# The first batch's keys and scores in another order, by key blocks, in a fused attention and adapter kernel

## The chip, the cores and the metric

The kernel runs on one core of a Trainium2 chip, as one program. The metric is the device time of one execution in microseconds (us). Engines named below: TensorE (PE in the profile, PEld for its weight loads), VectorE (DVE), ScalarE (ACT), GpSimd (POOL) and SyncE (SP), which only issues transfers. Each engine works through its own queue of instructions; semaphores order them against each other.

## The reference

Four images of 384 x 32 pixels with 128 channels are average-pooled by 4 x 4 patches and projected, which gives 768 keys that are also the values. 12,288 queries for each image attend to them. The result goes through a mixture of eight rank-16 adapters, of which each row uses its two best.

```python
def _attn_ref(q, kv, w_sr):
    kv_pool = kv.reshape(B, H // r, r, W // r, r, C).mean(axis=(2, 4))
    kv_flat = kv_pool.reshape(B, -1, C) @ w_sr
    k = v = kv_flat
    s = scale * (q @ k.transpose(0, 2, 1))
    s = s - s.max(-1, keepdims=True)
    a = np.exp(s)
    a /= a.sum(-1, keepdims=True) + 1e-09
    return (a @ v).astype(np.float32)

def _moe_ref(x, w_gate, A, B):
    logits = x @ w_gate
    topk = np.argpartition(-logits, K, axis=1)[:, :K]      # K = 2
    w = softmax of the two selected logits
    delta[row] += w[row, k] * ((x[row] @ A[e]) @ B[e])     # for the two experts e
    return x + delta
```

B = 4, C = 128, r = 4, q is 4 x 12,288 x 128, kv is 4 x 384 x 32 x 128, all fp32; the output is 49,152 x 128 fp32.

## The kernel before

**Chunks and slots.** The 49,152 queries are cut into 96 chunks of 512 (24 for each image, which the code calls a batch). The main loop (line 417) has a slot for each chunk k from 4 to 95. In slot k the scores of chunk k are computed in three pairs of key blocks, `scores(k, 0)` to `scores(k, 2)` (line 238): two bf16 matmuls of 128 x 512 into one of two PSUM buffers (`sg`), then ScalarE's exponential into `em[k]`. `attend(k, s)` (line 248) multiplies `em[k]` with the values `vx`, six matmuls of 137 columns for each of four row groups, into `acc`, of which there is one buffer (`ps_a`, line 62). `normalize` (line 256) reads `acc` on VectorE, a reciprocal and a multiply into `xn`. `top` and `route` (lines 276, 285) find the two best experts and their weights, with a tanh on ScalarE. Then a chunk enters the adapter stage: `transposes` of `xn`, `down`, `gate` on VectorE, transposes of `hg` one slot later, `up` and `finish` (the store, issued by SP) one slot after that. The dictionary `att` (line 400) says which chunks attend in which slot; from chunk 8 on chunk k attends in slot k + 1, and before that chunk 0 has slot 4, chunk 1 slot 5, and slots 6, 7 and 8 have two each. `enter` follows from it.

**The start.** Chunks 0 to 3 have their scores computed ahead of the loop (lines 369 to 386), between the steps that make the first batch's keys. The first batch's pixels come in thirds h = 0, 1, 2 of two key blocks each. A third is loaded by eight transfers of 256 KB on SP's queue, `load_kv(0, h, r, x)` (line 89), r the row inside a patch and x which of the two key blocks; before, the order is r outer, x inner. `pair_step` (line 173) adds two rows on VectorE (512 columns); `keys` (line 187) sums the rest of a patch by 16 accumulating fp32 transposes on TensorE and scales it out of PSUM by VectorE into `kpT`; `keys2` (line 203) projects with `w_sr` and VectorE casts the result to `kfT`; `values` (line 209) makes `vx`, with the eight gate logits as extra columns. In the loop of line 372 the four adds of a third come together, then its 16 transposes, and between them the scores of the third before and its values.

**Queries.** The queries of chunks 0 to 7 are loaded as fp32 and turned on TensorE by `turn_q(g, m, engine)` (line 107): four transposes and one cast of 512 columns out of PSUM by the engine named. Chunks 0 to 3 (g = 0) are cast by ScalarE, and so are chunks 4 to 7 (g = 1, lines 397 and 454). From chunk 8 on queries come by a casting transfer on POOL's queue (`cast_q`) and a transposing one on SP's (`load_qT`).

**Order.** Every instruction is marked with `keep`, so that it stays in program order on its engine. Small PSUM tiles (`mtile`, line 70) share two buffers, in turn. `part` (line 517) is an attention over some of the key blocks only; before, only the tail uses it.

Of the kernel before, what the change touches and what calls it, by code (L numbers as in the profile page):

```python
# [10 lines left out]
FP32 = mybir.dt.float32  # L11
BF16 = mybir.dt.bfloat16
U16 = mybir.dt.uint16
FP16 = mybir.dt.float16
AF = mybir.ActivationFunctionType
ALU = mybir.AluOpType
# [4 lines left out]
def kernel(  # L21
# [10 lines left out]
    nc = tc.nc  # L32
    P = 128
    B, N, C = q.tensor.shape
# [3 lines left out]
    J = NKV // P  # L38
    T = 512
    S = T // P  # L40
    GC = 4
    GT = GC * T
    VC = C + E
    VE = VC + 1
    NB = N // T
# [21 lines left out]
    def mm(*a, **k):  # L67
        return keep(nc.tensor.matmul(*a, **k))  # L68

    def mtile(shape, dtype=FP32, name="mb"):  # L70
        return ps_m.tile(shape, dtype, tag="mb", name=name)
# [52 lines left out]
    keep(nc.scalar.dma_start(w_gate_sb, moe_w_gate))  # L124
    load_q(0, 0, GC * S)
    for h in range(3):
        for r in range(4):
            for x in range(2):
                load_kv(0, h, r, x)
    for m in range(GC):  # L130
        load_q(1, m * S, m * S + S)
    b_f = const.tile([P, C], FP32)
# [22 lines left out]

    kfT, vx = {}, {}

    def prepare(b, adder):

        sums, rest = [], []  # L160

        def pool_step(h, step, lo, hi):
            t = kvr[b, h]
            if step < 3:
                u, v = t[:, 0].rearrange("p g c -> p (g c)"), t[:, step + 1].rearrange("p g c -> p (g c)")
            else:
                w = 2 * C if step == 3 else C
                u, v = t[:, 0, :, 0:w], t[:, 0, :, w:2 * w]
                keep(adder.tensor_tensor(u, u, v, op=ALU.add))  # L169
                return  # L170
            keep(adder.tensor_tensor(u[:, lo:hi], u[:, lo:hi], v[:, lo:hi], op=ALU.add))  # L171

        def pair_step(h, r, x):
            u, v = (kvr[b, h][:, r + i, x] for i in range(2))
            keep(adder.tensor_tensor(u, u, v, op=ALU.add))

        for h in range(3):
            if adder is nc.vector:
                sums.append([lambda h=h, r=r, x=x: pair_step(h, r, x)
                             for r in (0, 2) for x in range(2)])  # L180
                continue
            sums.append([lambda h=h, step=step, lo=lo: pool_step(h, step, lo, lo + 512)
                         for step in range(5) for lo in range(0, 1024 if step < 3 else 512, 512)])

        st = {}

        def keys(h):
            if h == 0:
                st["kpT"] = prep.tile([P, J, P], FP32, tag="kpT", name="kpT")
                kfT[b] = per_b.tile([P, J, P], BF16, tag="kfT", name="kfT")  # L190
            kpT = st["kpT"]
            ps = mtile([P, 2, P], name="kpT_ps")
            if adder is nc.vector:
                parts = [(r, i, c) for r in (0, 2) for i in range(2) for c in range(4)]
            else:
                parts = [(0, i, 0) for i in range(2)]
            for n, (r, i, c) in enumerate(parts):
                mm(ps[:, i], kvr[b, h][:, r, i, c * C:(c + 1) * C], id_f, is_transpose=True,
                   start=(n == 0), stop=(n == len(parts) - 1))
            keep(nc.vector.tensor_scalar(kpT[:, 2 * h:2 * h + 2], ps, 1.0 / 16.0, None,  # L200
                                         op0=ALU.mult))

        def keys2(h):
            kpT = st["kpT"]
            ps = mtile([P, 2, P], name="kfT_ps")
            mm(ps, w_sr_sb, kpT[:, 2 * h:2 * h + 2], start=True, stop=True)
            keep(nc.vector.tensor_copy(kfT[b][:, 2 * h:2 * h + 2], ps))

        def values(h):
            if h == 0:  # L210
                vx[b] = per_b.tile([P, J, VE], FP16, tag="vx", name="vx")
                keep(nc.vector.memset(vx[b][:, :, VC:VE], 1.0))
            ps = mtile([P, 2, VC], name="v_ps")
            for i in range(2):
                mm(ps[:, i], st["kpT"][:, 2 * h + i], wext, start=(i == 0), stop=(i == 1))
            keep(nc.vector.tensor_copy(vx[b][:, 2 * h:2 * h + 2, 0:VC], ps))
            if adder is not nc.vector:
                st["vb", h] = prep.tile([P, 2, C], BF16, tag="vb", name="vb")
                keep(nc.vector.tensor_copy(st["vb", h], ps[:, :, 0:C]))

        def turn(h):
            ps = mtile([P, 2, P], BF16, name="kfT_ps")
            for i in range(2):
                mm(ps[:, i], st["vb", h][:, i], id_bf, is_transpose=True,
                   start=(i == 0), stop=(i == 1))
            keep(nc.vector.tensor_copy(kfT[b][:, 2 * h:2 * h + 2], ps))

        for h in range(3):
            for f in (keys, keys2, values) if adder is nc.vector else (keys, values, turn):
                rest.append(lambda h=h, f=f: f(h))  # L230
        return sums, rest

# [133 lines left out]

    LA = 4

    for m in range(GC):
        turn_q(0, m, nc.scalar)  # L370
    sums, rest = prepare(0, nc.vector)
    for h in range(3):
        for item in sums[h]:
            item()
        rest[3 * h]()
        if h > 0:
            scores(2, h - 1)
        rest[3 * h + 1]()
        if h > 0:
            scores(3, h - 1)  # L380
            rest[3 * h - 1]()
        scores(0, h)
        scores(1, h)
    rest[8]()
    scores(2, 2)
    scores(3, 2)
    rest = []

    late = const.tile([P, 1], FP32)
    keep(nc.gpsimd.tensor_copy(late, q_f[1][:, GC * S - 1, 0:1]))  # L390
# [3 lines left out]
    keep(nc.vector.tensor_scalar(a_bf, a_f, 0.5, None, op0=ALU.mult))  # L394
    b_bf = const.tile([P, C], BF16)
    keep(nc.vector.tensor_copy(b_bf, b_f))
    turn_q(1, 0, nc.scalar)


    att = {LA: [0], LA + 1: [1], LA + 2: [2, 3], LA + 3: [4, 5], LA + 4: [6, 7]}  # L400
    for k in range(8, NCHUNK):
        att[k + 1] = [k]
    normed = {}
    for t, ks in att.items():
# [12 lines left out]
    for k in range(LA, NCHUNK):  # L417
        b, i = divmod(k, NB)
        ka = att.get(k, [])
        kx = enter.get(k, [])  # L420
        if k % GC == 0:
            g = k // GC
            if 2 <= g + 1 < B * NG:
                load_qT(g + 1)
            if 4 <= g + 2 < B * NG and g + 2 not in q_bf:
                cast_q(g + 2)
        if b + 1 < B:
            if i == 4:
                sums, rest = prepare(b + 1, nc.gpsimd)
            if 4 <= i < 16:  # L430
                h, j = divmod(i - 4, 4)
                load_kv(b + 1, h, j, None)

        def after_norm(kn):
            top(kn)
            if kn == first[kn] + size[kn] - 1:
                route(first[kn])

        kn = [n for n in att.get(k - 1, []) if normed[n] == k]
        if k == LA:  # L440
            for s in range(S):
                attend(0, s)
            ka = []
        scores(k, 0)
        while later:
            later.pop(0)()
        for n in kn:
            normalize(n)
        pairs = [(kx[j] if j < len(kx) else None, kh[j] if j < len(kh) else None)
                 for j in range(max(len(kx), len(kh)))]  # L450
        for x_, h_ in pairs[:1]:
            transposes(x_, h_)
        if k + 1 in range(GC + 1, 2 * GC):
            turn_q(1, (k + 1) % GC, nc.scalar)
        scores(k, 1)
        for u_ in ku:
            up(u_)
            finish(u_)
        for a_ in ka[:-1]:
            for s in range(S):  # L460
                attend(a_, s)
            normalize(a_)
            after_norm(a_)
        if ka and len(ka) == 1:
            attend(ka[0], 0)
        for n in kn:
            after_norm(n)
        scores(k, 2)
        for x_ in kx[:1]:
            down(x_)  # L470
            gate(x_)
        if rest and i in (14, 15, 16, 18, 19, 20, 21, 22, 23):
            rest.pop(0)()
        for a_ in ka[-1:]:
            for s in range(1 if len(ka) == 1 else 0, S):
                attend(a_, s)
        for x_, h_ in pairs[1:]:
            transposes(x_, h_)
        for x_ in kx[1:]:
            down(x_)  # L480
            gate(x_)
        ku = kh
        kh = kx
        if b + 1 < B and 10 <= i < 21:
            h, j = divmod(i - 10, 4)
            for _ in range((4, 3, 1, 0)[j]):
                sums[h].pop(0)()
# [24 lines left out]
    def fetch(which, k):  # L512
        sb = run.tile([P, S, P], BF16, tag="tt1", name="tt1")
        keep(nc.scalar.copy(sb, which[k]))
        which[k] = sb

    def part(k, o, js):
        for s in range(S):
            for j in js:
                mm(o[:, s, 0:VE], em[k][:, j, s * P:(s + 1) * P], vx[k // NB][:, j],  # L520
                   start=(j == 0 and s % 2 == 0), stop=(j == J - 1 and s % 2 == 1))

    def wide(o):
        return o.rearrange("p a b -> p (a b)")[:, 0:T].rearrange("p (s c) -> p s c", s=S)
# [147 lines left out]
```

## Time and profile before

| | us |
|---|---|
| three runs | 408.81, 409.08, 409.26; median 409.08 |
| the profiled run | 409.56, its span 407.6 |
| TensorE matmul busy | 379.6 (93%) |
| TensorE weight loads busy | 306.9 (75%) |
| VectorE busy | 324.5 (80%) |
| ScalarE busy | 293.1 (72%) |
| GpSimd busy | 170.7 (42%) |

The span is the time from the first to the last instruction of one profiled execution. Busy times overlap between engines. A line of a timeline gives the start, the time to the end of the last of the merged instructions, the engine, the line of the kernel (L68 is the helper behind every matmul), the operation, the tiles out<-in, the shapes, how many, and in brackets the time the engine stood idle before and what ended it. The granted clock of TensorE has a mean of 0.991 over the run.

### The profile page before, as it was taken

The page shows a single profiled execution, that of the slowest core. Times are in us where ns is not written, and L with a number is a line of the kernel's source. Part 1 is how long each engine was busy: PE and PEld are TensorE (multiplying, and loading weights), DVE is VectorE, ACT ScalarE, POOL GpSimd, SP SyncE. Part 2 cuts the span into 40 slices and gives each one's busy share as a digit, 9 for nine tenths or more (in the row PEclk, how much of TensorE's full clock was granted, in tenths as well). Part 3 has the DMA queues.
Part 4 walks back from the last instruction along what each step waited for, and adds up shares of the span by engine and source line. Part 5 has one row for each costly group of instructions (what it writes and reads, how often), then busy time and mean ns, then how long its engine had stood idle before and what let it go on. Part 6 is the DMA issues. An engine that isn't in the chain of part 4 may idle for free.

```text
span 407.6 us, 11369 instructions
## 1 busy us (share of the span) xinstructions
PE 379.6 (93%) x4514; PEld 306.9 (75%) x4589; DVE 324.5 (80%) x948; ACT 293.1 (72%) x346; POOL 170.7 (42%) x289
## 2 busy tenths in 40 slices
PE   3798899999999999999999999999999999898992
PEld 2556778788888788888888788878888878677781
DVE  2553678888888888989888888988988888887873
ACT  2389468767678777867778877876777877665772
POOL 0010128888512319879411319879311322123342
PEclk9999999999999999999999999999999999999996
DMA  8998568984855999994855979996756548252213
GB/s 297 366 265 245 137 156 214 285 210 124 182 130 105 307 172 336 295 219 138 168 130 117 363 103 344 287 225 145 156 131 149 138 130 156 79 138 97 79 53 132
DMA packets 71319, 76.45 MB, mean 188 GB/s; under 512 B 49921, under 2 KB 50433, under 8 KB 70785
## 3 DMA queue, kind: packets, MB, share of 16 engines
q1 hardware_dynamic: 70128, 63.98, 53.8%
q0 software_dynamic: 704, 11.54, 16.7%
q8 instruction: 36, 0.59, 0.6%
q10 hardware_dynamic: 432, 0.20, 0.2%
q14 instruction: 19, 0.15, 0.1%
HBM read 50.53 MB, written 36.70 MB: 214 GB/s over the span
## 4 chain that ended last, share of the span: by engine, by line
PE 82%; DVE 7%; ACT 3%; DMA 3%; issue 2%; SPq 1%; POOL 1%; ACTq 0%; DVEq 0%; POOLq 0%
PE acc L68 34%; PE sg L68 23%; PE tt_ps L68 10%; PE h_ps L68 6%; PE d_ps L68 5%; ACT em L246 2%; DVE rinv L258 1%; DVE xn L263 1%; DMA kvr<-in_kv_dram 1%; SPq L98 1%; DMA w_sr_sb<-in_w_sr_dram 1%; PE kpT_ps L68 1%; DVE tts L333 1%; PE v_ps L68 1%; DVE hg L347 1%
## 5 line engine op out<-in xcount | busy, mean ns | idle before, releaser
L246 ACT ACTIVATE em<-sg 128x1024 f16<-128x1024 f32 x288 | 279.1, 1023 | 92.1 <-PE sg L68 59.5
L68 PE MATMUL acc<-vx,em 128*128 128x137 f16 x2280 | 171.7, 224 | 1.7 <-DVE xn L263 1.6
L68 PE MATMUL sg<-qT,kfT 128*128 128x512 bf16 x501 | 154.7, 378 | 2.7 <-ACT em L246 2.2
L68 PEld LDWEIGHTS <-em 128*128 128x128 f16 x2304 | 149.6, 98 | 4.0 <-DVE xn L263 2.2
L68 PEld LDWEIGHTS <-tts 128*128 128x128 bf16 x740 | 56.4, 98 | 45.8 <-DVE tts L333 2.1
L293 POOL TENSOR_TENSOR over<-xn,srt 128x128 f32<-128x128 f32 (+2 forms) x62 | 21.4, 365 | 157.0 <-DVE srt L281 157.0
L347 DVE TENSOR_TENSOR hg<-h_ps,gw 128x512 bf16<-128x512 f32 x93 | 64.2, 691 | 13.2 <-POOL gw L315 7.6
L263 DVE TENSOR_TENSOR xn<-acc,rinv 128x544 f32<-128x544 f32 x95 | 68.8, 725 | 3.3
L333 DVE COPY tts<-tt_ps 128x1024 bf16<-128x1024 bf16 (+1 forms) x96 | 64.4, 671 | 3.6 <-PE tt_ps L68 3.6
L171 POOL TENSOR_TENSOR kvr<-kvr 128x512 f32<-128x512 f32 x54 | 66.7, 1271 | 0.0
L360 DVE TENSOR_TENSOR osb<-d_ps,xn 128x512 f32<-128x512 f32 x91 | 62.6, 691 | 0.5 <-PE d_ps L68 0.5
L68 PEld LDWEIGHTS <-kfT 128*128 128x128 bf16 x576 | 45.9, 97 | 6.0 <-issue 3.7
L68 PEld LDWEIGHTS <-xn 128*128 128x128 bf16 x384 | 29.4, 98 | 22.0 <-ACT xn L585 0.5
L258 DVE RECIPROCAL rinv<-acc 128x4 f32<-128x4 f32 x95 | 17.3, 182 | 32.5 <-PE acc L68 31.4
L68 PE MATMUL h_ps<-a_bf,tts 128*128 128x128 bf16 x372 | 36.0, 219 | 2.8 <-DVE tts L333 1.6
L68 PE MATMUL tt_ps<-id_bf,xn 128*128 128x128 bf16 x372 | 35.9, 219 | 1.5
L68 PE MATMUL d_ps<-b_bf,tts 128*128 128x128 bf16 x364 | 35.2, 219 | 2.3 <-DVE tts L333 1.3
L68 PE MATMUL tt_ps<-id_bf,hg 128*128 128x128 bf16 x368 | 35.6, 219 | 0.3 <-DVE hg L347 0.3
L281 DVE MAX8 srt<-xn 128x8 f32<-128x8 f32 x380 | 34.3, 153 | 0.2
L314 POOL TENSOR_TENSOR gw<-th,over 128x128 f32<-128x128 f32 (+2 forms) x31 | 12.0, 389 | 39.2 <-ACT th L312 39.1
L68 PEld LDWEIGHTS <-hg 128*128 128x128 bf16 x384 | 25.5, 98 | 2.5 <-issue 1.1
L169 POOL TENSOR_TENSOR kvr<-kvr 128x512 f32<-128x512 f32 (+1 forms) x18 | 18.1, 1006 | 0.9
(77 smaller groups left out, 174.8 us busy)
## 6 DMA issues: line engine op xcount, KB each, us to landing
out_dram<-osb SPq DMA_DIRECT2D x95, 256.0 KB, 3.3
kvr<-in_kv_dram SPq DMA_DIRECT2D x36, 512.0 KB, 6.3
qbf<-in_q_dram POOLq DMA_DIRECT2D x22, 512.0 KB, 6.1
kvr<-in_kv_dram SPq DMA_DIRECT2D x24, 256.0 KB, 5.4
qf<-in_q_dram SPq DMA_DIRECT2D x1, 1024.0 KB, 5.1
qf<-in_q_dram SPq DMA_DIRECT2D x4, 256.0 KB, 5.2
qT<-qbf SPq DMA_TRANSPOSE x22, 6.3
out_dram<-osb ACTq DMA_DIRECT2D x1, 128.0 KB, 3.1
```

Of the source, the lines that this page charges most:

```text
L68: return keep(nc.tensor.matmul(*a, **k))
L169: keep(adder.tensor_tensor(u, u, v, op=ALU.add))
L171: keep(adder.tensor_tensor(u[:, lo:hi], u[:, lo:hi], v[:, lo:hi], op=ALU.add))
L246: keep(nc.scalar.activation(em[k][:, 2 * r:2 * r + 2], ps, AF.Exp, bias=0.0, scale=scale))
L258: keep(nc.vector.reciprocal(ri, acc[k][:, :, VC]))
L263: keep(nc.vector.tensor_tensor(x, acc[k][:, :, 0:VC], ri.unsqueeze(2).broadcast_to([P, S, VC]), op=ALU.mult))
L281: keep(nc.vector.max(srt[k0][:, m, s], xn[k][:, s, C:VC]))
L293: keep(eng.tensor_tensor(d, lg, so[:, :, i].unsqueeze(2).broadcast_to([P, n, 8]), op=ALU.subtract))
L314: keep(eng.tensor_tensor(w[:, 0:n], th, mask, op=ALU.mult))
L333: keep(nc.vector.tensor_copy(sb[:, lo:hi], ps[:, lo:hi]))
L347: keep(nc.vector.tensor_tensor(hg[k].rearrange("p s (e r) -> p (s e) r", e=E), hp[k].rearrange("p s (e r) -> p (s e) r", e=E), gw[k0][:, m ...
L360: keep(nc.vector.tensor_tensor(osb, dp[k], xn[k][:, :, 0:C], op=ALU.add))
```

## The change

Seven things are done, all for the first batch.

1. The loads of the last third come with x outer and r inner; thirds 0 and 1 as before.
2. Third 0: `values_of(0, 0, ...)` stands right after scores(0,0) and (1,0), ahead of third 1's adds.
3. Third 1: the adds come in two halves; scores(2,0) and (3,0) stand between the two halves of the patch transposes.
4. Third 2 is made by columns: block 4 (x = 0) is added, transposed, scaled, projected and cast by itself, then block 5 (x = 1). Scores of the second pair stand between these steps.
5. The attention of chunk 0 is split by key blocks with `part`: blocks 0 to 3 between scores(2,2) and scores(3,2), blocks 4 and 5 behind scores(3,2), ahead of the loop.
6. So chunks attend one slot earlier: chunk 1 in slot 4, two chunks each in slots 5 and 6, and from chunk 6 on chunk k in slot k + 1. Chunks 0 to 3 enter the adapter stage in slots 5 to 8 instead of 6 to 9; from chunk 4 on nothing differs.
7. The casts of the queries of chunks 4 to 7 go from ScalarE to VectorE.

`prepare` loses its branch for VectorE; later batches compute as before.

```diff
-        for r in range(4):
-            for x in range(2):
-                load_kv(0, h, r, x)
+        for n in range(8):
+            load_kv(0, h, *((n // 2, n % 2) if h < 2 else (n % 4, n // 4)))
...
+    def values_of(b, h, kpT):
+        if h == 0:
+            vx[b] = per_b.tile([P, J, VE], FP16, tag="vx", name="vx")
+            keep(nc.vector.memset(vx[b][:, :, VC:VE], 1.0))
+        ps = mtile([P, 2, VC], name="v_ps")
+        for i in range(2):
+            mm(ps[:, i], kpT[:, 2 * h + i], wext, start=(i == 0), stop=(i == 1))
+        keep(nc.vector.tensor_copy(vx[b][:, 2 * h:2 * h + 2, 0:VC], ps))
+        return ps
...
+    def pair(h, x, r):
+        u, v = (kvr[0, h][:, r + i, x] for i in range(2))
+        keep(nc.vector.tensor_tensor(u, u, v, op=ALU.add))
+
+    def patches(ps, h, x, rs, first_, last_):
+        n = [(r, c) for r in rs for c in range(4)]
+        for i, (r, c) in enumerate(n):
+            mm(ps, kvr[0, h][:, r, x, c * C:(c + 1) * C], id_f, is_transpose=True,
+               start=(first_ and i == 0), stop=(last_ and i == len(n) - 1))
+
+    def pooled(ps, lo, hi):
+        keep(nc.vector.tensor_scalar(kpT0[:, lo:hi], ps, 1.0 / 16.0, None, op0=ALU.mult))
+
+    def project(lo, hi):
+        ps = mtile([P, 2, P], name="kfT_ps")[:, 0:hi - lo]
+        mm(ps, w_sr_sb, kpT0[:, lo:hi], start=True, stop=True)
+        keep(nc.vector.tensor_copy(kfT[0][:, lo:hi], ps))
...
-    for h in range(3):
-        for item in sums[h]:
-            item()
-        rest[3 * h]()
-        if h > 0:
-            scores(2, h - 1)
-        rest[3 * h + 1]()
-        if h > 0:
-            scores(3, h - 1)
-            rest[3 * h - 1]()
-        scores(0, h)
-        scores(1, h)
-    rest[8]()
-    scores(2, 2)
-    scores(3, 2)
+    ps = mtile([P, 2, P], name="kpT_ps")
+    for r in (0, 2):
+        for x in range(2):
+            pair(0, x, r)
+            patches(ps[:, x], 0, x, (r,), x == r == 0, x == 1 and r == 2)
+    pooled(ps, 0, 2)
+    project(0, 2)
+    scores(0, 0)
+    scores(1, 0)
+    values_of(0, 0, kpT0)
+    ps = mtile([P, 2, P], name="kpT_ps")
+    for x in range(2):
+        pair(1, x, 0)
+        patches(ps[:, x], 1, x, (0,), x == 0, False)
+    scores(2, 0)
+    scores(3, 0)
+    for x in range(2):
+        pair(1, x, 2)
+        patches(ps[:, x], 1, x, (2,), False, x == 1)
+    pooled(ps, 2, 4)
+    pair(2, 0, 0)
+    project(2, 4)
+    ps = mtile([P, P], name="kpT_ps")
+    patches(ps, 2, 0, (0,), True, False)
+    scores(0, 1)
+    scores(1, 1)
+    pair(2, 0, 2)
+    values_of(0, 1, kpT0)
+    pair(2, 1, 0)
+    patches(ps, 2, 0, (2,), False, True)
+    pooled(ps, 4, 5)
+    scores(2, 1)
+    ps = mtile([P, P], name="kpT_ps")
+    patches(ps, 2, 1, (0,), True, False)
+    project(4, 5)
+    pair(2, 1, 2)
+    patches(ps, 2, 1, (2,), False, True)
+    pooled(ps, 5, 6)
+    scores(3, 1)
+    project(5, 6)
+    scores(0, 2)
+    scores(1, 2)
+    values_of(0, 2, kpT0)
+    acc[0] = ps_a.tile([P, S, 256], FP32, tag="acc", name="acc")
+    scores(2, 2)
+    part(0, acc[0], range(4))
+    scores(3, 2)
+    part(0, acc[0], range(4, J))
...
-    turn_q(1, 0, nc.scalar)
+    turn_q(1, 0, nc.vector)
-    att = {LA: [0], LA + 1: [1], LA + 2: [2, 3], LA + 3: [4, 5], LA + 4: [6, 7]}
-    for k in range(8, NCHUNK):
+    att = {LA - 1: [0], LA: [1], LA + 1: [2, 3], LA + 2: [4, 5]}
+    for k in range(6, NCHUNK):
         att[k + 1] = [k]
...
-        if k == LA:
-            for s in range(S):
-                attend(0, s)
-            ka = []
...
-            turn_q(1, (k + 1) % GC, nc.scalar)
+            turn_q(1, (k + 1) % GC, nc.vector)
```

More of the change, by code (lines that the diff above doesn't have):

```diff
@@ L156, with prepare @@
     kfT, vx = {}, {}
-    def prepare(b, adder):
+    def values_of(b, h, kpT):
[7 more added lines that the diff above has]
+        return ps
+    def prepare(b):
         sums, rest = [], []
@@ L168, in pool_step @@
                 u, v = t[:, 0, :, 0:w], t[:, 0, :, w:2 * w]
-                keep(adder.tensor_tensor(u, u, v, op=ALU.add))
+                keep(nc.gpsimd.tensor_tensor(u, u, v, op=ALU.add))
                 return
[L171 to L175, printed above, removed]
+            keep(nc.gpsimd.tensor_tensor(u[:, lo:hi], u[:, lo:hi], v[:, lo:hi], op=ALU.add))
         for h in range(3):
[L178 to L181, printed above, removed]
             sums.append([lambda h=h, step=step, lo=lo: pool_step(h, step, lo, lo + 512)
@@ L192, in keys @@
             ps = mtile([P, 2, P], name="kpT_ps")
[L193 to L199, printed above, removed]
+            for i in range(2):
+                mm(ps[:, i], kvr[b, h][:, 0, i, 0:C], id_f, is_transpose=True,
+                   start=(i == 0), stop=(i == 1))
             keep(nc.vector.tensor_scalar(kpT[:, 2 * h:2 * h + 2], ps, 1.0 / 16.0, None,
                                          op0=ALU.mult))
[L203 to L207, printed above, removed]
-        def values(h):
[L210 to L219, printed above, removed]
+        def values(h):
+            ps = values_of(b, h, st["kpT"])
+            st["vb", h] = prep.tile([P, 2, C], BF16, tag="vb", name="vb")
+            keep(nc.vector.tensor_copy(st["vb", h], ps[:, :, 0:C]))
         def turn(h):
@@ L228, in prepare @@
         for h in range(3):
-            for f in (keys, keys2, values) if adder is nc.vector else (keys, values, turn):
+            for f in (keys, values, turn):
                 rest.append(lambda h=h, f=f: f(h))
@@ L367 @@
     LA = 4
+    kpT0 = prep.tile([P, J, P], FP32, tag="kpT", name="kpT")
+    kfT[0] = per_b.tile([P, J, P], BF16, tag="kfT", name="kfT")
+    def pair(h, x, r):
[6 more added lines that the diff above has]
+               start=(first_ and i == 0), stop=(last_ and i == len(n) - 1))
@@ new lines, in pooled, with part @@
+    def pooled(ps, lo, hi):
[4 more added lines that the diff above has]
+        keep(nc.vector.tensor_copy(kfT[0][:, lo:hi], ps))
+    def part(k, o, js):
+        for s in range(S):
+            for j in js:
+                mm(o[:, s, 0:VE], em[k][:, j, s * P:(s + 1) * P], vx[k // NB][:, j],
+                   start=(j == 0 and s % 2 == 0), stop=(j == J - 1 and s % 2 == 1))
@@ L369 @@
     for m in range(GC):
         turn_q(0, m, nc.scalar)
-    sums, rest = prepare(0, nc.vector)
-    for h in range(3):
-        for item in sums[h]:
-            item()
-        rest[3 * h]()
-        if h > 0:
-            scores(2, h - 1)
-        rest[3 * h + 1]()
-        if h > 0:
-            scores(3, h - 1)
-            rest[3 * h - 1]()
-        scores(0, h)
-        scores(1, h)
-    rest[8]()
+    ps = mtile([P, 2, P], name="kpT_ps")
[3 more added lines that the diff above has]
+            patches(ps[:, x], 0, x, (r,), x == r == 0, x == 1 and r == 2)
@@ L385 @@
     scores(2, 2)
+    part(0, acc[0], range(4))
     scores(3, 2)
-    rest = []
+    part(0, acc[0], range(4, J))
+    sums, rest = [], []
     late = const.tile([P, 1], FP32)
@@ L428 @@
             if i == 4:
-                sums, rest = prepare(b + 1, nc.gpsimd)
+                sums, rest = prepare(b + 1)
             if 4 <= i < 16:
@@ L515, in fetch @@
         which[k] = sb
[L517 to L521, printed above, removed]
     def wide(o):
```

## The prediction

> **What bounds the kernel now.** I read the busy times by stretch first. They say where TensorE is short of work.
>
> ```profile
> 26.00:30.40 4.40, 3.81 (x22) 2.39 (x22) 1.58 (x5) 4.21 (x5) 1.13 (x2) 1.00 0.70 119
> 30.40:38.00 7.60, 6.49 (x62) 4.71 (x62) 1.95 (x10) 6.87 (x10) 0.00 (x0) 1.00 0.99 221
> 46.00:54.00 8.00, 7.16 (x95) 6.04 (x96) 5.10 (x17) 4.05 (x6) 2.44 (x7) 1.00 0.42 68
> 100.00:120.00 20.00, 19.79 (x245) 16.31 (x248) 17.76 (x52) 15.13 (x18) 7.20 (x12) 1.00 0.79 170
> ```
>
> Columns: stretch, length, busy us (instructions) of PE, PEld, DVE, ACT, POOL, then granted clock, DMA share, GB/s. From 62 us on TensorE is 99% busy; between 26 and 30 ScalarE is the full engine (4.21 of 4.40), from 30 to 54 TensorE is about 90% busy. The clock is 1.00 throughout. So the change can only move what lies before about 60 us, and its worth is how much earlier TensorE gets through the same work. Second, the order of time in the start:
>
> ```profile
> 14.52 0.43 DVE L207 CAST kfT<-kfT_ps 128x256 bf16<-128x256 f32 x1 [0.85 <-PE kfT_ps L68]
> 14.86 1.28 DVE L175 TENSOR_TENSOR kvr<-kvr 128x512 f32<-128x512 f32 x2
> 21.55 0.45 DVE L216 CAST vx<-v_ps 128x272 f16<-128x272 f32 x1 [0.44 <-PE v_ps L68]
> 21.91 2.49 DVE L175 TENSOR_TENSOR kvr<-kvr 128x512 f32<-128x512 f32 x4
> 26.36 0.42 DVE L207 CAST kfT<-kfT_ps 128x256 bf16<-128x256 f32 x1 [0.79 <-PE kfT_ps L68]
> ...
> 26.79 4.69 ACT L246 ACTIVATE em<-sg 128x1024 f16<-128x1024 f32 x5 [0.19 <-PE sg L68]
> 30.12 0.60 PE L68 MATMUL qT_ps<-id_f,qf 128*128 128x128 f32 x4
> 30.56 1.66 PE L68 MATMUL acc<-vx,em 128*128 128x137 f16 x24
> 31.33 0.63 ACT L116 CAST qT<-qT_ps 128x512 bf16<-128x512 f32 x1
> 32.05 0.59 PE L68 MATMUL sg<-qT,kfT 128*128 128x512 bf16 x2
> ```
>
> VectorE carries the chain: adds, scale, key cast, value cast, in program order. The last key blocks are ready at 26.78, five exponentials follow, and slot 4 begins at 32.05 with scores(4,0); the query cast that it needs hides under attention 0. Third, TensorE's own waits after that:
>
> ```profile
> 35.16 0.59 PE L68 MATMUL sg<-qT,kfT 128*128 128x512 bf16 x2 [0.81 <-ACT em L246]
> 42.77 1.67 PE L68 MATMUL acc<-vx,em 128*128 128x137 f16 x24 [0.38 <-DVE xn L263]
> 48.89 1.66 PE L68 MATMUL acc<-vx,em 128*128 128x137 f16 x24 [0.38 <-DVE xn L263]
> 51.82 0.59 PE L68 MATMUL sg<-qT,kfT 128*128 128x512 bf16 x2 [0.39 <-ACT em L246]
> 55.17 1.04 PE L68 MATMUL acc<-vx,em 128*128 128x137 f16 x14 [0.38 <-DVE xn L263]
> ```
>
> Slots 4 and 5 wait for ScalarE; slots with two attentions wait for the one accumulator, which normalize must read first. Measured between starts, each of these gaps is some 0.17 larger than the bracket, since ends are modelled.
>
> **Prices, from these rows.** An add lasts 0.69 and the next starts 0.604 later (four in 2.49). VectorE out of PSUM: 256 columns 0.42, 272 0.45, 128 0.29 (the copy of wT); a successor starts 0.09 before the end. Four patch transposes: 0.43 of TensorE, 0.60 to the last end; eight, 1.04. A projection of 256 columns 0.70. Scores: 0.43, 0.59 to the end. Exponential 1.02, every 0.917. Values 0.47, 0.63 to the end. Attention 24 x 0.062 = 1.49. A hop between engines 0.03 to 0.06.
> Not in the trace: the 128-column projection (between 0.35, half, and 0.70; I take 0.40, two of the value matmuls, 0.279 + 0.117) and a 512-column cast by VectorE (between ScalarE's 0.61 and the 0.725 of the 544-column multiply; 0.69, by the slope from 256 to 272 columns and the 0.69 of the 512-column adds from PSUM).
> [...]
>
> **Start.** To 14.95 nothing changes: loads, adds and transposes of third 0 keep their order.
> Third 1. Value cast 0 now stands ahead of its adds on VectorE. Scores(0,0), (1,0) issue 15.00 to 15.86, values end 16.51, cast 16.55 to 17.00. The adds start at 16.91 instead of 14.86 and end at 19.41 (before 18.69; the last load landed at 17.93). Scores (2,0), (3,0) take TensorE 18.75 to 19.61, the last eight transposes end 20.67, scale 20.70 to 21.12, projection 21.18 to 21.88, key cast done 22.34: before 21.08, **+1.26**. ScalarE has four exponentials done by 21.4 and then waits.
> Third 2, by columns. Its loads, issued 13.41 to 17.92 and landing 5.1 to 5.2 later, are in by 23.1; VectorE reaches each add after its landing, so the new load order is worth nothing. Add (x0) 21.04, the other 22.25 to 22.94. Then VectorE waits 1 us: scores (0,1), (1,1) 22.40 to 23.26, values end 23.89, value cast to 24.36. Add (x1) to 24.96, scale of block 4 to 25.16, four transposes to 25.64, projection 25.66 to 26.06, cast 26.09 to 26.37. The last add is queued behind that cast: 26.28 to 26.97. Transposes end 27.62, scale 27.94, projection 28.39, cast **28.71: +1.93**. With the bounds of the short projection 0.1 less to 0.6 more.
> To slot 4. Scores(3,1), kept behind those transposes, exponentiate from 28.1. Scores(0,2) at 28.77, exponential 29.41 to 30.43; scores(2,2) needs that buffer: 30.49 to 30.92; 16 attention matmuls to 31.91; scores(3,2) to 32.34; the other eight to 32.84; query transposes end 33.44; cast 33.47 to 34.16. Nothing is left on TensorE behind the transposes, so the cast that was free is now 0.7 on the path. Scores(4,0) at 34.21: **+2.16** against 32.05.
>
> **Slots 4 to 11.** Scores(12,0) is at 67.71, so this took 35.66. By slot 12 the same work is done either way. Before: slots of 3.11, 3.39, 5.72, 6.12, 6.28, then 3.68 each.
> After: slot 4 has attention 1: 1.28 scores + 0.43 query + 1.45 = 3.16, with 0.1 of loose ends 3.26; ScalarE needs 2.9 and stops being the limit. Slot 5 equals old slot 6, 5.72. Slot 6 equals old slot 7 plus query transposes 0.43, less 0.18 of wait that they fill: 6.37. Slot 7 has one attention: 3.62 of work + 0.55 for the tanh that holds exp(6,2), as at 51.82 = 4.17. Slot 8 3.68. Slots 9, 10, 11 lack a chunk's transposes and down, then transposes, then up: 3.24, 3.46, 3.46. Sum 33.36: **-2.30**. The saving is one double slot's two waits (1.1) and the starving of slots 4 and 5 (1.4 + 0.2).
> The three other casts on VectorE (0.69 each) sit ahead of a normalize that starts a microsecond later, so I cost them at nothing; without that cover up to 0.6 each. Tanh 0 now stands between exp(4,1) and exp(4,2); its argument is ready within 0.1 of exp(4,1)'s end, and scores(5,1) has 0.5 to spare.
> On SP, the store of chunk 0 is now ahead of the second transposing load: that moves from 36.58 to about 52. It landed 9.5 after issue, so by 62, needed at 67; nothing, unless it is over 5 later. The casting loads on POOL and batch 1's adds keep their slots.
> **Sum.** +2.16 - 2.30 = -0.14 on the span of 407.6. The profiled run took 409.56, the median 409.08; with that 1.48 between span and median kept, **408.9**.
>
> **Rivals.** *A: the start costs nothing.* If VectorE's waits for the two value casts and the short cast (1.55 + 1.0 + 0.9) are filled, slot 4 begins at 32.05 and only the 2.30 counts: 406.8. For it: the last load lands at 23.1, and 23.1 + 0.69 + 0.60 + 0.29 + 0.40 + 0.29 is 25.4, so data allow it. Against: the trace keeps program order on VectorE everywhere, as where gw waits 4.12 for tanh.
> *B: slower, the accumulator.* VectorE's query cast lands in front of normalize in slots 4 to 6, and the single accumulator makes attention wait. It decides once the cast starts less than 0.69 ahead of an attention's end; price 3 x 0.6 = 1.8, so +1.66 and 410.7. For: VectorE is the busy engine there (5.42 of 8.00 from 38 to 46). Against: the cast is ready 1 us ahead by the walk.
> *C: the new load order is not done or pays:* not above 0.2 either way, since VectorE is late.
>
> **Numbers.** 0.2% is 0.82 us here, about what a measurement tells from no change. Forecast 0.53, own range 407.9 to 409.9 (unknown prices -0.1 to +0.6, slots within 0.4): of it 0.11 faster, 0.33 same, 0.09 slower. A 0.25, nearly all faster (0.24); B 0.22, 0.20 slower and 0.02 same. So faster 0.35, same 0.36, slower 0.29. Range 406.6 to 410.9: A and B inside, a tenth outside either end.
>
> **What would show it.** Key casts ending near 22.3 and 28.7; an add starting near 16.9; scores(4,0) near 34.2 with a wait for VectorE's cast; slot 12 near 67.6; one attention less waiting for xn. Wrong if the last key cast ends before 27, or if TensorE waits for xn in slot 4.

## The result, and the profile after

| | before | changed |
|---|---|---|
| median of 4 runs each, us | 409.05 (408.81 to 409.26) | 409.13 (408.82 to 409.47) |
| profiled run, its span | 409.56, 407.6 | 409.47, 407.6 |
| VectorE busy | 324.5 | 327.4 |
| ScalarE busy | 293.1 | 291.6 |

The ratio is 1.0002, with a 95% interval of 0.9985 to 1.002: no change that can be told. The forecast was 408.9, with "same" at 0.36 hardly ahead of "faster" at 0.35. What matters is whether it came out even for the stated reason, a loss in the start against a gain of the same size behind it.

The busy times by stretch of the changed kernel, columns as before:

```profile
26.00:30.40 4.40, 3.25 (x19) 1.89 (x20) 1.47 (x4) 2.02 (x3) 1.01 (x2) 1.00 1.01 190
30.40:38.00 7.60, 6.60 (x68) 5.08 (x68) 4.04 (x16) 5.97 (x8) 0.00 (x0) 1.00 0.83 195
46.00:54.00 8.00, 7.18 (x94) 5.93 (x93) 5.96 (x22) 4.56 (x6) 2.43 (x7) 1.00 0.41 61
54.00:62.00 8.00, 7.89 (x97) 6.29 (x97) 5.99 (x20) 6.10 (x7) 1.20 (x3) 1.00 0.63 116
100.00:120.00 20.00, 19.77 (x245) 16.37 (x249) 17.75 (x51) 14.86 (x17) 7.66 (x12) 1.00 0.78 166
```

Between 26 and 30 ScalarE is now busy for 2.02 of 4.40 us, where it was full (4.21), and TensorE has 3.25 instead of 3.81. Part of this is that this trace runs 0.8 us later from the first key cast on (below), so the fixed stretch shows an earlier piece of the work; the waits in the timeline show that the start has also become emptier. From 54 on TensorE is 99% busy, some 8 us earlier than before (7.51 of 8.00 in the same stretch). The timeline of the changed kernel in the start:

```profile
15.34 0.42 DVE L372 CAST kfT<-kfT_ps 128x256 bf16<-128x256 f32 x1 [0.85 <-PE kfT_ps L68]
...
17.36 0.45 DVE L164 CAST vx<-v_ps 128x272 f16<-128x272 f32 x1 [1.56 <-PE v_ps L68]
17.71 2.49 DVE L358 TENSOR_TENSOR kvr<-kvr 128x512 f32<-128x512 f32 x4
...
22.70 0.43 DVE L372 CAST kfT<-kfT_ps 128x256 bf16<-128x256 f32 x1 [0.20 <-PE kfT_ps L68]
...
24.72 0.44 DVE L164 CAST vx<-v_ps 128x272 f16<-128x272 f32 x1 [1.00 <-PE v_ps L68]
...
26.80 0.29 DVE L372 CAST kfT<-kfT_ps 128x128 bf16<-128x128 f32 x1 [0.83 <-PE kfT_ps L68]
27.00 0.68 DVE L358 TENSOR_TENSOR kvr<-kvr 128x512 f32<-128x512 f32 x1
...
29.30 0.29 DVE L372 CAST kfT<-kfT_ps 128x128 bf16<-128x128 f32 x1 [0.58 <-PE kfT_ps L68]
...
34.14 0.69 DVE L118 CAST qT<-qT_ps 128x512 bf16<-128x512 f32 x1 [2.40 <-PE qT_ps L68]
...
34.89 0.60 PE L68 MATMUL sg<-qT,kfT 128*128 128x512 bf16 x2 [0.79 <-DVE qT L118]
```

Three idle stretches of VectorE ahead of casts, 1.56, 1.00 and 0.83 us, each with adds queued behind the cast whose data had landed (two adds' pixels of third 1 by 14.85, all of third 2 by 22.59); and TensorE's wait of 0.79 for the query cast. In this trace the whole start is 0.8 later than in the trace of before already at the first key cast (15.34 against 14.52), which the change does not touch. So the stages are measured from the end of that cast (us):

| | first key cast ends | from there: third 1's | last key cast | scores(4,0) | slots 4 to 11 | scores(12,0) |
|---|---|---|---|---|---|---|
| before | 14.95 | 6.13 | 11.83 | 17.10 | 35.66 | 52.76 |
| changed | 15.76 | 7.37 | 13.83 | 19.13 | 33.66 | 52.79 |
| forecast | 14.95 | 7.39 | 13.76 | 19.26 | 33.36 | 52.62 |

A loss of 2.03 and a gain of 2.00. Rows that these stages rest on, before (third 1's key cast and scores(12,0)), then changed (scores(12,0)):

```profile
20.65 0.43 DVE L207 CAST kfT<-kfT_ps 128x256 bf16<-128x256 f32 x1 [0.79 <-PE kfT_ps L68]
...
67.71 0.59 PE L68 MATMUL sg<-qT,kfT 128*128 128x512 bf16 x2
```

```profile
68.55 0.59 PE L68 MATMUL sg<-qT,kfT 128*128 128x512 bf16 x2
```

Behind scores(12,0) the changed kernel gains 0.15 more in slots 12 to 27 (61.48 against 61.63), which was not forecast and whose cause was not followed; all kernels with the new slots have it. From slot 28 to 95 the two agree to 0.01. The waits that are left in the slots of the changed kernel, in TensorE's timeline (the second attention is cut by the end of the view's window):

```profile
42.38 1.67 PE L68 MATMUL acc<-vx,em 128*128 128x137 f16 x24 [0.38 <-DVE xn L247]
...
48.75 1.42 PE L68 MATMUL acc<-vx,em 128*128 128x137 f16 x20 [0.38 <-DVE xn L247]
...
51.68 0.59 PE L68 MATMUL sg<-qT,kfT 128*128 128x512 bf16 x2 [0.39 <-ACT em L230]
```

Two waits for the accumulator instead of three, the one for the held exponential as before, and none for ScalarE in slots 4 and 5 (0.81 at 35.16 before).

### The profile page after: what moved, and what is told of

Read it like the earlier page. It is cut to its first block, busy times and chain, and to the rows that moved or that the text cites. A ratio compares the mean times of both kernels' runs of the same rounds, so it can differ in the third digit from the quotient of the medians.

```text
span 407.6 us, 11377 instructions
## 1 busy us (share of the span) xinstructions
PE 379.5 (93%) x4516; PEld 307.8 (76%) x4591; DVE 327.4 (80%) x955; ACT 291.6 (72%) x342; POOL 171.1 (42%) x289
## 4 chain that ended last, share of the span: by engine, by line
PE 81%; DVE 7%; DMA 4%; issue 2%; ACT 2%; SPq 2%; POOL 1%; ACTq 0%; DVEq 0%; POOLq 0%
PE acc L68 33%; PE sg L68 23%; PE tt_ps L68 10%; PE h_ps L68 6%; PE d_ps L68 5%; SPq L98 2%; DVE rinv L242 1%; DMA w_sr_sb<-in_w_sr_dram 1%; ACT em L230 1%; DMA kvr<-in_kv_dram 1%; DVE xn L247 1%; DVE hg L331 1%; DVE tts L317 1%; DMA b_f<-in_moe_B_dram 1%; PE v_ps L68 1%
```

## The experiments

Two theories were set against each other: mine, that the new start costs about 2.2 and the new slots give about 2.3, the two being independent; and the plain one, that neither does anything. Then the start's cost was taken apart. Each kernel was timed in five rounds beside the kernel of before.

**The slots alone, in two forms.** Both keep the start of before.

```diff
 # both, against before
-    att = {LA: [0], LA + 1: [1], LA + 2: [2, 3], LA + 3: [4, 5], LA + 4: [6, 7]}
-    for k in range(8, NCHUNK):
+    att = {LA - 1: [0], LA: [1], LA + 1: [2, 3], LA + 2: [4, 5]}
+    for k in range(6, NCHUNK):
...
-            turn_q(1, (k + 1) % GC, nc.scalar)
+            turn_q(1, (k + 1) % GC, nc.vector)
 # the first, ahead of the loop
-    turn_q(1, 0, nc.scalar)
+    for s in range(S):
+        attend(0, s)
+    turn_q(1, 0, nc.vector)
 # the second, ahead of the loop
-    turn_q(1, 0, nc.scalar)
+    turn_q(1, 0, nc.vector)
+    for s in range(S):
+        attend(0, s)
```

> The start of before, unchanged; chunk 0 attends whole ahead of the loop, then the first query transposes, and from slot 4 on all is as in the changed kernel (attentions one slot up, query casts on VectorE). Theory (two halves: the new start costs about 2.2 us, the new slots give about 2.3): scores(4,0) 0.9 later than before (near 32.9), because nothing covers the first query cast, then the slots give 2.3: near 407.6 (-1.4). Rival 1 (the slots give nothing, the start costs nothing): 409.1 or, with the cast exposed, 409.9. Rival 2 (the slots give only 1): 408.9.

Measured 407.17 against 409.09 (ratio 0.9949, 0.9935 to 0.9962), -1.92 where -1.4 was expected.

> As the run before it, but the first query transposes stand ahead of chunk 0's attention, so that VectorE casts under it. Theory: scores(4,0) near 32.05 as before, slots 4 to 11 take 33.4 to 33.7 instead of 35.7: near 406.8 (-2.3), and 0.9 below the run with the cast exposed. Rival 1: 409.1. Rival 2: 408.1.

Measured 406.29 against 409.09 (0.9932, 0.992 to 0.9945), -2.80 where -2.3 was expected. It is faster than both kernels. The stages of the two runs give -1.48 and -2.27 up to scores(12,0) and 0.14 more in slots 12 to 27; the remaining 0.3 to 0.4 of each median lies in no stage that was followed. Its timeline around the query cast:

```profile
29.80 0.60 PE L68 MATMUL qT_ps<-id_f,qf 128*128 128x128 f32 x4
30.44 0.69 DVE L118 CAST qT<-qT_ps 128x512 bf16<-128x512 f32 x1 [1.09 <-PE qT_ps L68]
...
31.73 0.59 PE L68 MATMUL sg<-qT,kfT 128*128 128x512 bf16 x2
```

The scores have no bracket: the cast ended at 31.13, under the attention. Slots 4 to 11 took 33.66 and 33.64 us. So the slots give their 2.0 with any start, and the exposed cast costs 0.88 (0.9 forecast). "The slots give nothing" falls.

**The start alone.** The changed kernel with the old slots: chunk 0's `part` calls out, `att` and the ScalarE query casts as before, chunk 0 attending in slot 4.

> The new start (block-major, last third by columns, new load order) without chunk 0's split attention; slots and query casts as before the change. Theory: last key cast near 28.7 instead of 26.8, scores(4,0) near 33.8, slots 4 to 11 unchanged at 35.7: near 410.8 (+1.7). Rival 1 (the start costs nothing): 409.1. Rival A of the prediction (the start would even be earlier): below 409.

Measured 411.44 against 409.09 (1.0059, 1.0046 to 1.0071). The last key cast ended 13.83 after the first, as in the changed kernel, scores(4,0) 18.67, against 17.10 before: +1.57, and slots 4 to 11 took 35.65. "The start costs nothing" falls, as does rival A. The measured +2.35 is above the +1.6 of the stages. Between the two runs that were traced it is 1.88 (411.44 - 409.56), since that of before lay 0.47 above its median. Of the 1.88, 0.44 is a longer end of the program (18.85 from the last slot's transposes to the span's end, against 18.41 in the trace of before), and a first key cast that ends 0.10 earlier takes that off again.

**The exposed cast.** The changed kernel with the first query transposes moved up.

```diff
     values_of(0, 2, kpT0)
+    turn_q(1, 0, nc.vector)
     acc[0] = ps_a.tile([P, S, 256], FP32, tag="acc", name="acc")
     scores(2, 2)
...
-    turn_q(1, 0, nc.vector)
```

> The changed kernel with only the first query transposes and their VectorE cast moved up, between the values of the last third and scores(2,2), where TensorE waits for an exponential. Theory: the 0.8 wait of scores(4,0) for the cast goes, and the 0.43 of transposes partly fills a wait: scores(4,0) about 1.2 earlier, near 407.9 (-1.2 against before). Rival (the cast's wait is covered by ScalarE, which is not done either): no change from the changed kernel, 409.1.

Measured 407.97 against 409.09 (0.9973, 0.9962 to 0.9984); scores(4,0) 17.86 after the first key cast instead of 19.13, 1.27 earlier. So ScalarE was not a second limit behind the cast, and the rival falls.

**VectorE's order.** The next four runs leave out the transposing query loads, so that moves in the start alone are compared against a base of the same kind:

```diff
-        t = qpool.tile([P, GT], BF16, tag="qT", name="qT")
-        keep(nc.sync.dma_start(t.rearrange("c (j p) -> c j p", p=P),
-                               q_bf[g].rearrange("(p j) c -> p (j c)", p=P), transpose=True))
-        qT[g] = t
+        qT[g] = qT[g % 2]
```

> The changed kernel without the transposing query loads: chunks 8 to 95 use the queries of chunks 0 to 7 again, so that part of the computation is left out. It is the base for the runs that move instructions in the start, which lies ahead of the first such load's use. Theory: TensorE sets the pace and these loads are hidden, so the same 409.1 within 0.4, with scores(4,0) 19.2 to 19.5 after the end of the first key cast. Rival (the load that was moved past chunk 0's store costs something in slots 8 to 12): below 408.5.

Measured 408.60 against 409.27 (0.9984, 0.9975 to 0.9992), 0.1 outside the 0.4 that was allowed; the time alone does not decide about the rival. Its stages are those of the changed kernel to 0.01 (13.84, 19.13, 33.66), so the load that was moved past chunk 0's store costs nothing in the slots: the rival falls there. In the changed kernel that load was issued at 53.73, took 7.5 to land, and was needed near 68.5. The 0.67 by which this run is below before is not the start's; 0.35 of it is in slots 12 to 95 (0.15 of that the changed kernel has too), the rest was not followed. Three moves against this base:

```diff
 # first move: adds of third 1 ahead of value cast 0
+    for x in range(2):
+        pair(1, x, 0)
     values_of(0, 0, kpT0)
     ps = mtile([P, 2, P], name="kpT_ps")
     for x in range(2):
-        pair(1, x, 0)
         patches(ps[:, x], 1, x, (0,), x == 0, False)
 # second move: adds of third 2 ahead of value cast 1 and of block 4's key cast
+    pair(2, 1, 0)
     values_of(0, 1, kpT0)
-    pair(2, 1, 0)
...
+    pair(2, 1, 2)
     project(4, 5)
-    pair(2, 1, 2)
```

> As the base without late queries (408.6), with one move: the first two adds of third 1 ahead of the value cast of third 0 on VectorE. Theory: third 1's key cast ends 6.15 after the first third's instead of 7.4, and everything behind it comes 1.26 earlier: near 407.3. Rival (the cost of the start is in the column-wise third 2 alone, this one is absorbed there): 408.6.

Measured 407.35 (0.9953 of before, 0.9939 to 0.9966), 1.25 below the base. Third 1's key cast ended 5.85 after the first, the last one 12.33, scores(4,0) 17.62: 1.51 earlier, more than the 1.26 of the theory. So the cost of VectorE's order in third 1 is shown, but the close match of the time is in part luck.

> As the base without late queries (408.6), with the other move: one add of third 2 ahead of the value cast of third 1, one ahead of the key cast of block 4. Theory: the last key cast comes 1.75 earlier: near 406.9. Rival (the doubled short projections and casts of the columns are the cost, not the order): 408.2 to 408.6.

Measured 407.37 (0.9951, 0.9939 to 0.9964), 1.23 below the base, 0.5 short of the forecast; in its trace the last key cast came 1.65 earlier (12.19) and scores(4,0) too (17.48). The 0.4 between trace and time was not located. The doubled short projections and casts are still there, so the order, not they, made up the 1.65.

> As the base (late queries left out), with three moves: the first two adds of third 1 ahead of the value cast of third 0; the adds of third 2 ahead of the value cast of third 1 and of the key cast of block 4; the first query transposes and their VectorE cast ahead of scores(2,2). Theory (the start's cost is VectorE's order and the exposed cast): last key cast near 25.8 to 26, limited by the last load near 23, scores(4,0) near 30.0, slots 4 to 11 unchanged: 4.2 to 4.9 below the base, near 404.5. Rival (TensorE or ScalarE becomes the limit in the start, so that the parts don't add): 2 to 3 below the base.

Measured 404.51 (0.9884, 0.9868 to 0.9899), 4.09 below the base. VectorE's timeline in it:

```profile
14.87 0.42 DVE L369 CAST kfT<-kfT_ps 128x256 bf16<-128x256 f32 x1 [0.85 <-PE kfT_ps L68]
15.21 1.28 DVE L355 TENSOR_TENSOR kvr<-kvr 128x512 f32<-128x512 f32 x2
...
16.89 0.45 DVE L161 CAST vx<-v_ps 128x272 f16<-128x272 f32 x1 [0.36 <-PE v_ps L68]
17.25 1.28 DVE L355 TENSOR_TENSOR kvr<-kvr 128x512 f32<-128x512 f32 x2
...
21.06 1.28 DVE L355 TENSOR_TENSOR kvr<-kvr 128x512 f32<-128x512 f32 x2
22.74 0.44 DVE L161 CAST vx<-v_ps 128x272 f16<-128x272 f32 x1 [0.39 <-PE v_ps L68]
...
23.38 0.68 DVE L355 TENSOR_TENSOR kvr<-kvr 128x512 f32<-128x512 f32 x1
24.27 0.29 DVE L369 CAST kfT<-kfT_ps 128x128 bf16<-128x128 f32 x1 [0.20 <-PE kfT_ps L68]
...
25.68 0.29 DVE L369 CAST kfT<-kfT_ps 128x128 bf16<-128x128 f32 x1 [0.58 <-PE kfT_ps L68]
```

The waits of 1.56, 1.00 and 0.83 ahead of casts have become 0.36, 0.39 and 0.20, because adds whose data is there fill them. The last key cast ends at 25.97 (10.68 after the first), scores(4,0) starts at 30.00. The parts add: 1.51 + 1.65 + 1.27 is 4.43, the trace has 4.42, and the rival falls. In times they give 1.25 + 1.23 + 1.20 = 3.68 against 4.09, which intervals of about half a microsecond on each side allow.

All ten by the same measure (us from the end of the first key cast; the last four without late queries):

| kernel | scores(4,0) | slots 4 to 11 | time against before |
|---|---|---|---|
| before | 17.10 | 35.66 | |
| changed | 19.13 | 33.66 | +0.08 |
| slots only, cast exposed | 17.62 | 33.66 | -1.92 |
| slots only, cast covered | 16.85 | 33.64 | -2.80 |
| start only | 18.67 | 35.65 | +2.35 |
| changed, query moved up | 17.86 | 33.64 | -1.12 |
| base without late queries | 19.13 | 33.66 | -0.67 |
| base, adds ahead of value cast 0 | 17.62 | 33.66 | -1.92 |
| base, adds of third 2 ahead | 17.48 | 33.66 | -1.90 |
| base, all three moves | 14.71 | 33.64 | -4.76 |

The two middle columns form two groups: the start sets one, the slots the other, and neither moves the other.

Not measured: the load order of third 2 alone, the query casts of slots 4 to 6 on ScalarE, and the moves of adds, each alone or all three moves together, with the late queries in place. For all three an estimate is 405.0, the changed kernel's 409.13 less the 4.09 that they gave against the base.

## Why the prediction was right, step by step

- *Third 1 (+1.26 forecast).* Measured 7.37 - 6.13 = 1.24 by VectorE's order; the run that puts the adds first removes it, and 0.28 more (5.85).
- *Third 2 by columns (+1.93 at the last key cast).* Measured 13.83 - 11.83 = 2.00. The short projection, taken as 0.40 between 0.35 and 0.70, took 0.39 and 0.49; the 128-column cast 0.29 as taken. That TensorE's fp32 rows (four transposes 0.60 to 0.66, the projection of 256 columns 0.70), VectorE's 0.604 spacing (four adds in 2.49) and the hops (most 0.03 to 0.06) carry over to an order that no trace had shown is why the walk came out within 0.1.
- *To slot 4 (+2.16).* Measured +2.03. The exposed cast was named (0.7 on the path) and took 0.69 on VectorE, with a wait of 0.79 in front of the scores. The four casts on VectorE took 0.681 to 0.692; ScalarE's eight had taken 0.580 to 0.667 in the trace of before.
- *Slots (-2.30).* Measured -2.00. Slots 4 to 8 were 3.26, 5.73, 6.38, 4.22, 3.68 against 3.26, 5.72, 6.37, 4.17, 3.68. The term that was mis-sized is slots 9 to 11: 3.31, 3.54, 3.54 instead of 3.24, 3.46, 3.46. A missing group of four transposes or adapter matmuls was taken at 0.22, the distance at which such a group issues when measured by starts; it saved 0.14 to 0.19. That is 0.23 of the 0.30. The sentence that breaks the saving down (1.1 + 1.4 + 0.2) adds up to 2.7, not to the 2.30 of the slots: with one double slot only one wait for the accumulator went (three before, two after, 0.55 each between starts), and the one for the held exponential stayed.
- *Costed at nothing.* The three casts in the slots made nobody wait: the query casts at 35.97, 39.54 and 46.26 ended 0.8 or more ahead of the next attention's end. Tanh 0 ran at 37.52, right behind its exponential. The moved load had 7 us in hand.
- *Rival A* (a start that costs nothing) had the bound right: the loads allow a last key cast at 25.4, and the run with all moves reached 25.97. It erred in supposing that the changed order would use it. *Rival B* (the accumulator waits for the query casts) did not come: one such wait fewer than before. *Rival C* (the load order): VectorE came to those adds after their data in the changed kernel. By the landings in its trace the old order would not have held it either: the first add would have had its data at 19.32 and started at 21.82, the second at 21.89 and started at 23.04, and the last load of the third landed at 22.59. That is argued; no run isolates it.
- *The sum.* -0.14 forecast; +0.03 at scores(12,0) by the traces, +0.08 by the medians. The start cost 0.13 less than forecast and the slots gave 0.30 less; that these two misses partly cancel in the sum is luck. That a loss and a gain of about 2 cancel is the mechanism as forecast.

## What to carry to other kernels

An engine that carries a chain in program order needs more than less work: look at what stands behind each instruction that waits. Here a cast that waits for TensorE held adds whose data had landed, three times, for about 3 us in all by the traces (1.51 + 1.65; 2.5 by the times); moving those adds ahead of the casts, with no work saved, won it back. A change of several parts that comes out even should be split before it is dropped: this one was +2 and -2, and the half worth keeping (attentions a slot earlier, with the query cast under the attention) gave 2.8 us alone by the medians, 2.4 of it in stages that the traces show.

## What the runs showed of the hardware

**The start varies.** The end of the first key cast lay between 14.69 and 15.98 in the ten traces, with the same instructions ahead of it. In the changed kernel's trace the fourth add waited longer for its load (1.22 against 0.33), and most of the transposes were slow:

```profile
10.96 3.06 PE L68 MATMUL kpT_ps<-id_f,kvr 128*128 128x128 f32 x16
12.35 0.69 DVE L358 TENSOR_TENSOR kvr<-kvr 128x512 f32<-128x512 f32 x1 [1.22 <-DMA kvr<-in_kv_dram]
14.06 0.42 DVE L367 TENSOR_SCALAR kpT<-kpT_ps 128x256 f32<-128x256 f32 x1 [1.02 <-PE kpT_ps L68]
```

From the add's end at 13.04 to the scale is 1.02, where the trace of before had 0.75 (12.49 to 13.24). The single transposes tell why (shortest, median and longest in ns). The first ten in the changed kernel's trace, then all sixteen in that of before:

```profile
L68 PE MATMUL kpT_ps<-id_f,kvr x10: 417/417/473, 11.0 to 12.9; 128*128 128x128 f32 x10
```

```profile
L68 PE MATMUL kpT_ps<-id_f,kvr x16: 272/272/331, 11.0 to 12.9; 128*128 128x128 f32 x16
```

From 13.31 on they take 272 or 273 in the changed kernel's trace too. Each trace's record of the granted clock begins with 1.00 at about the point where its transposes become short: 13.25 here, 10.77 before, and between 10.46 and 13.59 in the ten. What the clock was ahead of that is not recorded; the longer transposes suggest that it was lower. Of the ten, the four with the latest such point (13.59, 13.25, 13.21, 12.24) have the four latest key casts. Why it varies is not shown. Single traces of such a kernel are to be compared from a point behind that.

**So does the end.** TensorE reached the last slot's transposes 0.69 later than in the trace of before (389.88 and 389.19), yet both spans are 407.6. The granted clock fell to 0.50 at 399.89 us in the trace of before and at 402.37 in the other, as the last matmuls show, before first:

```profile
401.33 0.84 PE L68 MATMUL sg<-b_bf,tt 128*128 128x128 bf16 x6
```

```profile
401.96 0.50 PE L68 MATMUL sg<-b_bf,tt 128*128 128x128 bf16 x6
```

The fall goes with the point above: in both traces it comes 389.12 us after the record of 1.00 begins, and in the ten it comes 382.29, 385.71 or 389.12 after it, in steps of 3.41. So a trace whose clock comes up late can also keep it longer at the end.

And the last store of 128 KB took 2.5 us before, 2.1 after, 2.7 with the start alone and 1.9 in the other seven; why was not found. The first key cast's end and the stretch from the last slot's transposes to the span's end, added, differ by up to 1.3 us among the ten traces, more than the sum of this change.
